# A three-layer fp32 kernel on one core: the prologue of its attention is reordered, and its weight conversions come 16 slots later

## The chip, the cores and the metric

One core of a Trainium2 chip runs one program with three layers in it. The metric is device time in microseconds of one execution; lower is better. The profile names the engines PE (TensorE, matmuls) with PEld (its weight loads), DVE (VectorE), ACT (ScalarE), POOL (GpSimd) and SP (SyncE, which here does nothing but issue DMAs). SPq and ACTq are DMAs issued from SyncE's and from ScalarE's instruction stream.

## The reference, cut to what matters

Inputs are fp32; the weights of the second layer, `w_in` and `w_out`, arrive as 8-byte floats, of which the kernel makes fp32 itself.

```python
# q, k, v: (2, 8, 768, 64); centroids: (8, 16, 64)
q_assign = np.argmax(einsum(normalised q, normalised centroids), axis=-1)   # 16 clusters
k_assign = ...                                                             # the same for k
mask = q_assign[:, :, :, None] == k_assign[:, :, None, :]
scores = np.where(mask, scale * q @ k.T, -1e9)
scores = scores - scores.max(-1, keepdims=True)
attn = np.exp(scores); attn /= attn.sum(-1, keepdims=True) + 1e-9
x = (attn @ v) reshaped to (1536, 512)
x = (s * relu(x @ w_in) ** 2 + b) @ w_out        # d_ff 2048
# then a mixture of 8 experts on x, one expert a row, d_ff 1024
```

## The kernel before, in words

**Attention, head by head.** There are 16 heads of 768 rows. A head is prepared in these steps, each a small function inside `attention`:

- `load` (L117): SyncE loads q and k (and, apart, v) of 192 KB each.
- `split` (L145): ScalarE rounds q or k to the fast fp32r type (the high part, L150), GpSimd (for head 0 VectorE) subtracts to get the low part (L152).
- `trans` (L157): three TensorE transposes into the PSUM bank `t`, one ScalarE copy out of it (L168); four such groups a head, two for k and two for q. After the second of each, SyncE copies the high half into `ka` or `qa` by DMA (L170).
- `sims_mm` and `sims_a` to `sims_e` (L174 to L203): similarities with the centroids on TensorE into one PSUM bank, then six VectorE instructions that find the cluster of each row.
- `masks` (L205): a VectorE transpose turns the clusters into extra rows of `qa` and `ka` (tile `ot`, L208). In heads 0 and 1 the four pieces are copied by ScalarE (L216) and VectorE (L218), two each; from head 2 on SyncE sends them by four DMAs (L212, L214).
- `M` (L220): 12 score matmuls a head, each followed by a VectorE maximum over its 384 columns (L224). In head 0 they rotate over five PSUM banks, later over two.
- `mneg`, `mrow` (L228, L232): the negated row maxima, turned into a row by a TensorE matmul (`mr`, L235), a ScalarE copy (`mrs`, L237) and a small SyncE DMA into `qa` (L238).

Only with that row in `qa` can the head's own 12 score pairs `Sx` start (L247, L248; the exponentials on ScalarE, L249; two PSUM banks `s0`, `s1`), then `V` (attn times v), `presum` (GpSimd adds the exponentials) and the normalisation.

**What sets the order.** Every function is put into a list with a time in slots, `at(t, f, ...)`; the list is sorted by that time, and each engine's instructions are pinned to the order that comes out. A slot is no measure of time, only a rank. Head j's first score matmul `Sx` has slot 12j, so 12 slots are a head; all its other steps have an offset from there in the table `TIMES` (L31). Thus M of head j stands at slots 12j - 17.4 to 12j - 6.4 and its maxima row at 12j - 3.5 (head 0: -5.6). `HEAT` (L35) puts idle bf16 matmuls (`heat`, L1133) into the prologue, and two more behind each M of head 0.

**The hooks of the second layer** (`Moe.hooks`, L393) stand in the same list. `fetch` (L401) loads the raw weights of blocks 0, 1 and 2, 1 MB each in two DMAs, from ScalarE's stream, at slots 5.3, 17.3 and 29.3 (`FETCH`). `conv_steps` (L416) converts block f in steps at slots 36f + 12 + `CONV`: two ScalarE absolute values (L422), then seven VectorE instructions on integers; the last step, at 36f + 43.2, loads the raw block f + 3 into the buffers just freed. Of these loads, block 3's is issued by ScalarE and those of blocks 4, 5 and 6 by SyncE. Block 4 is converted at slots 176.2 and after. `early` (L396) fills constants and loads two scalars at slot 6.3; `unit` and `project` prepare the expert embedding.

The second layer (`moe1`) and the experts follow, with their matmuls in three passes of fp32r parts.

Of the kernel before, what the change touches and what calls it, by code (L numbers as in the profile page):

```python
# [9 lines left out]
F32 = mybir.dt.float32  # L10
# [5 lines left out]
AF = mybir.ActivationFunctionType  # L16
# [5 lines left out]
P = 128  # L22
# [3 lines left out]
HS = S // 2  # L26
# [2 lines left out]
MASK = float(2 ** 33)  # L29
GUARD = 1e-9  # L30
TIMES = dict(load=-49, loadv=-18, split=(-42, -40), trans=(-36.6, -35.6, -33.6, -32.6), sims=-30.53, simv=(-26.5, -26.5, -26.5, -22.52, -22.52, -22.51),  # L31
             M=-17.4, mneg=-5.7, mrow=-3.5, V=(5.45, 5.45, 9.45, 9.45, 13.45, 13.45), presum=3.0, norm=(14.5, 25.47, 29.5, 29.5, 29.5))
ENDS = {14: (14.5, 21.47, 22.4, 23.4, 24.4), 15: (14.5, 14.6, 14.7, 14.8, 14.9)}
WARM = -26
HEAT = ((-41, 7), (-30.5, 6), (-22, 6))  # L35
SETUP, FETCH = 6.3, (5.3, 17.3, 29.3)
CONV = (3.2, 7.2, 11.2, 15.2, 19.2, 23.2, 27.2, 31.2)
F, DM, TC = 2048, 512, 512
NF, KD, NTT = F // P, DM // P, TC // P
E, F2 = 8, 1024  # L40
NWA = 5
# [50 lines left out]


def attention(ax, tc, cst, q, k, v, cen, xt, hooks, embed):
    nc = tc.nc
    ident, identr, ones, desc, cc, ps = cst.ident, cst.identr, cst.ones64, cst.desc, cst.cc, cst.ps
    io = ax.enter_context(tc.tile_pool(name="io", bufs=3))
    w1 = ax.enter_context(tc.tile_pool(name="w1", bufs=2))
# [4 lines left out]
    NSET, NPB = 4, 8  # L103
    qa = [ab.tile([P, S], F32R, name=f"qa{i}") for i in range(NSET)]
    ka = [ab.tile([P, S], F32R, name=f"ka{i}") for i in range(NSET)]
# [66 lines left out]
    si, sm = {}, {}  # L172
# [31 lines left out]

    def masks(j):  # L205
        i = j % NSET
        ot = w1.tile([P, HS], F32, name="ot", tag="ot")
        nc.vector.transpose(out=ot, in_=si.pop(j))  # L208
        for g in range(4):
            da, w = (qa, ka)[g // 2][i], slice(g % 2 * HS, (g % 2 + 1) * HS)  # L210
            if j >= NSET:
                nc.sync.dma_start(out=da[64:64 + NC_, w].bitcast(F32), in_=ot[32 * g:32 * g + NC_])  # L212
            elif j > 1:
                nc.sync.dma_start(out=da[64:96, w].bitcast(F32), in_=ot[32 * g:32 * g + 32])  # L214
            elif g % 2 == 0:
                nc.scalar.activation(out=da[64:96, w], in_=ot[32 * g:32 * g + 32], func=AF.Copy)  # L216
            else:
                nc.vector.tensor_copy(da[64:96, w], ot[32 * g:32 * g + 32])  # L218

    def M(j, r, c):  # L220
        i = j % NSET
        pp = ps([P, HS], "M", f"M{c}" if j else ("M0", "M1", "s0", "s1", "s2")[(2 * r + c) % 5])
        nc.tensor.matmul(pp, qa[i][0:80, r * P:(r + 1) * P], ka[i][0:80, c * HS:(c + 1) * HS])  # L223
        nc.vector.tensor_reduce(out=mxt[j % 2][:, r, c:c + 1], in_=pp, axis=AX.X, op=ALU.max)  # L224
# [90 lines left out]
    c = w1.tile([P, D], F32, name="c", tag="c")  # L315
# [8 lines left out]
    n = order.mark()  # L324
# [12 lines left out]
    def at(t, f, *a):  # L337
        ops.append((t, len(ops), f, a))

    at(WARM, lambda: nc.scalar.activation(out=cst.warm, in_=cst.ones64[0:1, 0:1], func=AF.Exp, scale=0.0))  # L340
    at(-31, cluster, ch)
    for t, n in HEAT:
        at(t, cst.heat, n, "pv")
    at(-30, lambda: [nc.sync.dma_start(out=ka_[96:97, :].bitcast(F32), in_=one) for ka_ in ka])
    for t, f in hooks:
        at(t, f)
    T = TIMES
    for j in range(NH):
        o = 12 * j
        if j >= 3:  # L350
            at(o + T["load"], load, j, "qk")
            at(o + T["loadv"], load, j, "v")
        if j > 0:
            for i in range(2):
                at(o + T["split"][i], split, j, i)
        for i in range(4):
            at(o + T["trans"][i], trans, j, "kq"[i // 2], i % 2)
        at(o + T["sims"], sims_mm, j)
        for i, f in enumerate((sims_a, sims_b, sims_c, sims_d, sims_e, masks)):
            at(o + T["simv"][i], f, j)  # L360
        for r in range(NR):
            for c in range(2):
                at(o + T["M"] + 2 * r + c, M, j, r, c)
                if j == 0:
                    at(o + T["M"] + 2 * r + c, cst.heat, 2, "pv")
        at(o + T["mneg"], mneg, j)
        at(o + T["mrow"] if j else -5.6, mrow, j)
        for t in range(NR):
            for c in range(2):
                at(o + 2 * t + c, Sx, j, t, c)  # L370
            at(o + T["V"][t], V, j, t)
            at(o + 2 * t + T["presum"], presum, j, t)
        for i, f in enumerate((pv_out, sums, norm_a, norm_b, norm_c)):
            at(o + ENDS.get(j, T["norm"])[i], f, j)
    for t, _, f, a in sorted(ops, key=lambda x: x[:2]):
        n = order.mark()
# [4 lines left out]
class Moe:  # L381
# [11 lines left out]
    def hooks(self, ms, mb):  # L393
        nc = self.nc

        def early():  # L396
            for i, t in enumerate((ms, mb)):
                nc.sync.dma_start(out=self.sb[:, i:i + 1], in_=t.rearrange("(o n) -> o n", o=1).to_broadcast([P, 1]))
            self.setup()

        def fetch(f):  # L401
            self.loaded[f] = self.load_f64(f, nc.scalar)

        self.loaded, self.wT, self.wraw, self.running = {}, {}, {}, {}
        out = [(-27, self.length), (SETUP, early), (-16.6, self.unit), (SETUP + 9, self.project)] + [(t, lambda f=f: fetch(f)) for f, t in enumerate(FETCH)]
        for f in range(NWA):
            for n, t in enumerate(CONV):
                out.append((36 * f + 12 + t if f < NWA - 1 else 176.2 + n, lambda f=f: next(self.steps(f), None)))
        return out

    def steps(self, f):
# [4 lines left out]
    def conv_steps(self, f, wide=False):  # L416
        nc = self.nc
        r = self.loaded.pop(f)
        t = self.w32(f, U32)
        u = [self.ps([P, DM], "cv", "ab"[a]).bitcast(U32) if wide else t[:, a] for a in range(2)]  # L420
        for a in range(2):
            nc.scalar.activation(out=t[:, a].bitcast(F32), in_=r[a][:, :, 1].bitcast(F32), func=AF.Abs)  # L422
        yield
        s = t.rearrange("p a (w o) -> p o (a w)", o=2)
        nc.vector.tensor_scalar(out=s.bitcast(F32), in0=s.bitcast(F32), scalar1=CLAMP_LO, scalar2=CLAMP_HI, op0=ALU.max, op1=ALU.min)
        yield
        shift = dict(scalar1=5, scalar2=2, op0=ALU.logical_shift_left, op1=ALU.logical_shift_right)
        if wide:
            for a in range(2):
                nc.vector.tensor_scalar(out=u[a], in0=t[:, a], **shift)  # L430
        else:
            nc.vector.tensor_scalar(out=s, in0=s, **shift)
        yield
        for a in range(2):
            nc.vector.scalar_tensor_tensor(out=u[a], in0=r[a][:, :, 1], scalar=0xC0000000, in1=u[a], op0=ALU.bitwise_and, op1=ALU.bitwise_or)
            yield
            nc.vector.scalar_tensor_tensor(out=t[:, a], in0=r[a][:, :, 0], scalar=29, in1=u[a], op0=ALU.logical_shift_right, op1=ALU.bitwise_or)
            yield
        self.wT[f] = t
        if f + 3 < NF:  # L440
            self.loaded[f + 3] = self.load_f64(f + 3, nc.scalar if f + 3 < NWA - 1 else nc.sync)
        yield

    def pools(self):
# [12 lines left out]
    def ps(self, shape, name, tag):  # L457
        return self.cst.ps(shape, name, dict(a="pv", b="sm", y0="t", y1="s0", y2="s1", y3="s2").get(tag, tag))
# [124 lines left out]
    def moe1(self, xt):  # L583
# [4 lines left out]
        for c in range(self.chunks):  # L588
# [4 lines left out]
            def up(f):  # L593
# [4 lines left out]
                if final:  # L598
                    self.load_expert(f + 1)
                    if f in PRE0:  # L600
                        z = PRE0.index(f)
                        with self.after(*tail):
                            self.pre0[z] = self.half(self.wraw[0, z], 0, nc.gpsimd, False)
                hp = self.ps([P, TC], "hp", f"M{f % 2}")
                self.up_mm(hp, *wu, lambda k: x[k // 2][:, k % 2], lambda k: x[2 + k // 2][:, k % 2])
# [434 lines left out]
    def prep(self, xr):  # L1040
# [12 lines left out]
        return xh, xl  # L1053

    def block(self, y, args, w, pre, hooks, wd=None, g0=None):
        nc = self.nc
        xh, xl, off, _ = args
# [5 lines left out]
        def up(f):  # L1063
            with ExitStack() as behind:
# [5 lines left out]
                if f not in wd:  # L1070
                    wd[f] = self.half(w[f], 1, nc.vector)
            hp = self.ps([P, T], "hp", f"M{f % 2}")
            if xl is None:
# [79 lines left out]
@with_exitstack  # L1153
def tile_kernel(ctx, tc, q, k, v, cen, w_in, w_out, ms, mb, emb, tau, w1, w2, out):
    nc = tc.nc
    cst = consts(ctx, tc)
    xp = ctx.enter_context(tc.tile_pool(name="xp", bufs=1))
    xt = [xp.tile([P, KD, TC], F32, name="xt", tag=f"xt{i}") for i in range(NT // TC)]
    sb = cst.pool.tile([P, 2], F32, name="sb")
    moe = Moe(ctx, tc, cst, w_in, w_out, sb, emb, tau, w1, w2, out)  # L1160

    with ExitStack() as ax:
        attention(ax, tc, cst, q, k, v, cen, xt, moe.hooks(ms, mb), moe.embed)
    moe.pools()
    moe.xp = xp
    moe.moe1(xt)
    moe.spare = [xp.tile([P, KD, TC], dt, name="spare", tag=f"xt{i}") for i, dt in enumerate((F32R, F32R, F32))]
    moe.experts()
# [26 lines left out]
```

## Time and profile before

| what | value |
|---|---|
| times of three runs | 810.01, 814.52, 817.02 us; median 814.52 us |
| the profiled execution | 812.13 us |
| its span, first to last instruction | 810.3 us |
| mean granted TensorE clock over the span | 0.971 |
| busy PE / DVE / ACT / POOL | 764.7 / 521.3 / 422.0 / 347.6 us |
| first score matmul of head 0, of head 15 | 35.85 us, 274.74 us |
| last score matmul of the attention | 288.81 us |

The span is what the trace shows; 1.83 us of the profiled execution's time lie around it. Busy time is an average over stages with different limits. Matmuls are pipelined and their ends are modelled, so a busy TensorE is not necessarily one at its peak. In the views below, the text in brackets behind an instruction is the idle time of its engine just before it and what ended that.

### The profile page before, as it was taken

What the parts mean: (1) busy time and instruction counts of PE and PEld (TensorE: products, weight loads), DVE (VectorE), ACT (ScalarE), POOL (GpSimd) and SP (SyncE); (2) the same over time, 40 slices, a digit from 0 to 9 for tenths busy, and PEclk for the clock granted to TensorE, in tenths of its full rate; (3) what the DMA queues carried; (4) which work ended last, traced back from release to release, by engine and by line L of the source; (5) the groups of instructions that cost most, each with busy time, mean ns of one, the idle gap of its engine ahead of it and who ended that gap; (6) DMA issues with size and microseconds to landing.
All of it is one profiled execution on the core that took longest, in us unless ns stands there. A gap on an engine that the chain in (4) does not pass through costs nothing. (4 is left out here: it accounts for less than half of the span.)

```text
span 810.3 us, 12231 instructions
## 1 busy us (share of the span) xinstructions
PE 764.7 (94%) x4193; PEld 578.5 (71%) x4193; DVE 521.3 (64%) x1087; ACT 422.0 (52%) x841; POOL 347.6 (43%) x277
## 2 busy tenths in 40 slices
PE   7799999898998889999999999989999999999994
PEld 3456555554555458888788887868879998989883
DVE  5769789795995779994353542556447545757750
ACT  5355465554553665645435553445437545756651
POOL 2067766675684655445344544437042202220000
PEclk9899999998998999999999999989999999999998
DMA  5155423424331205521000042254132754876600
GB/s 149 50 148 171 126 69 87 141 75 120 76 81 58 61 22 159 183 74 45 8 1 1 1 155 79 81 205 156 66 117 69 255 178 139 245 248 227 213 17 23
DMA packets 75470, 88.73 MB, mean 110 GB/s; under 512 B 7445, under 2 KB 58549, under 8 KB 75008
## 3 DMA queue, kind: packets, MB, share of 16 engines
q1 hardware_dynamic: 68704, 69.67, 28.2%
q0 software_dynamic: 4000, 13.90, 5.4%
q10 hardware_dynamic: 2688, 4.19, 1.7%
q8 instruction: 40, 0.66, 0.3%
q14 instruction: 38, 0.31, 0.1%
HBM read 70.57 MB, written 7.34 MB: 96 GB/s over the span
## 5 line engine op out<-in xcount | busy, mean ns | idle before, releaser
L531 POOL TENSOR_TENSOR wl<-w,wh 128x512 fp32r<-128x512 f32 x96 | 123.2, 1308 | 130.5 <-ACT wh L529 127.9
L249 ACT ACTIVATE pt<-S 128x384 f32<-128x384 f32 x192 | 91.7, 490 | 120.3 <-PE S L248 115.7
L224 DVE TENSOR_REDUCE mx<-M 128x1 f32<-128x384 f32 x192 | 101.8, 551 | 50.8 <-PE M L223 48.7
L260 POOL TENSOR_TENSOR acc<-acc,pt 128x768 f32<-128x768 f32 x61 | 106.1, 1739 | 6.5 <-ACT pt L249 4.1
L552 PE MATMUL hp<-x,wh 128*128 128x512 f32 x384 | 105.9, 397 | 0.5 <-ACT wh L529 0.5
L552 PE MATMUL hp<-x,spare 128*128 128x256 f32 x732 | 96.1, 284 | 2.0 <-PEq L987 1.7
L552 PEld LDWEIGHTS hp<-x,spare 128*128 128x128 f32 x732 | 92.7, 190 | 6.9 <-issue 4.1
L560 PE MATMUL y<-wd,gg 128*128 128x512 f32 x360 | 93.2, 394 | 0.0
L608 DVE SCALAR_TENSOR_TENSOR hp<-hp,sb,t 128x512 f32<-128x512 f32 x48 | 36.3, 757 | 75.3 <-ACT t L607 75.2
L247 PE MATMUL S<-qa,ka 97*128 97x384 f32 x192 | 72.7, 379 | 12.7 <-DMA qa<-mrs 11.0
L223 PE MATMUL M<-ka,qa 80*128 80x384 f32 x192 | 79.4, 414 | 3.5 <-DVE mx L224 2.2
L552 PEld LDWEIGHTS hp<-x,wh 128*128 128x128 f32 x384 | 71.2, 189 | 15.5 <-ACT wh L529 1.2
L268 PE MATMUL pv<-pt,vn 128*64 128x385 f32 x384 | 77.3, 526 | 0.0
L560 PE MATMUL y<-wh,gh 128*128 128x512 f32 x192 | 75.3, 392 | 0.0
L560 PE MATMUL y<-wl,gh 128*128 128x512 f32 x192 | 75.2, 392 | 0.0
L545 DVE TENSOR_TENSOR wd<-w,wd 128x512 fp32r<-128x512 f32 x64 | 43.3, 686 | 44.4 <-ACT wd L544 41.0
L560 PEld LDWEIGHTS y<-wd,gg 128*128 128x128 f32 x360 | 63.7, 189 | 10.1 <-DVE gg L1084 0.2
L1036 POOL DMA_INDIRECT row<-rows,idx x24 | 28.0, 1166 | 94.1 <-PE tp L1048 50.8
L248 PE MATMUL S<-qb,kb 128*128 128x384 f32 x192 | 66.9, 349 | 0.0
L607 ACT ACTIVATE t<-hp 128x512 f32<-128x512 f32 x48 | 28.8, 599 | 72.1 <-PE hp L552 72.1
L223 PEld LDWEIGHTS M<-ka,qa 80*128 80x128 f32 x192 | 37.1, 194 | 37.8 <-DVE su L296 8.1
L560 PE MATMUL y<-wh,gl 128*128 128x512 f32 x192 | 59.5, 391 | 0.0
(269 smaller groups left out, 1363.2 us busy)
## 6 DMA issues: line engine op xcount, KB each, us to landing
w<-in_moe_w_dram SPq DMA_DIRECT2D x128, 256.0 KB
raw<-in_moe_w_in_dram SPq DMA_DIRECT2D x12, 512.0 KB
raw<-in_moe_w_out_dram SPq DMA_DIRECT2D x12, 512.0 KB
qn<-in_q_dram SPq DMA_DIRECT2D x16, 192.0 KB
kn<-in_k_dram SPq DMA_DIRECT2D x16, 192.0 KB
vn<-in_v_dram SPq DMA_DIRECT2D x16, 192.0 KB
ka<-kb SPq DMA_DIRECT2D x16, 192.0 KB
qa<-qb SPq DMA_DIRECT2D x16, 192.0 KB
```

The lines of the kernel that those rows point to most:

```text
L223: nc.tensor.matmul(pp, qa[i][0:80, r * P:(r + 1) * P], ka[i][0:80, c * HS:(c + 1) * HS])
L224: nc.vector.tensor_reduce(out=mxt[j % 2][:, r, c:c + 1], in_=pp, axis=AX.X, op=ALU.max)
L247: nc.tensor.matmul(pp, ka[i][0:97, t * P:(t + 1) * P], qa[i][0:97, w], start=True, stop=False)
L248: nc.tensor.matmul(pp, kb[i][:, t * P:(t + 1) * P], qb[i][:, w], start=False, stop=True)
L249: exps.setdefault((j, t), []).append(nc.scalar.activation(out=p[:, c, 0:HS], in_=pp, func=AF.Exp, scale=0.125).ins)
L260: eng.tensor_tensor(out=acc[j][-1], in0=acc[j][-1], in1=p[:, :, 0:HS], op=ALU.add)
L268: together(tc, [lambda c=c: nc.tensor.matmul(pv_t[j][c * 64:c * 64 + 64, :], io_t["v", j][:, t, :], p[:, c, :], start=t == 0, stop=t == NR ...
L531: eng.tensor_tensor(out=wl[:, a], in0=w[:, a], in1=wh[:, a].bitcast(F32), op=ALU.subtract)
L545: eng.tensor_tensor(out=t[:, 1], in0=w[:, a], in1=t[:, 0].bitcast(F32), op=ALU.subtract)
L552: self.nc.tensor.matmul(hp, a[:, k * P:(k + 1) * P], b(k), start=n == 0, stop=n == 3 * KD - 1)
L560: self.nc.tensor.matmul(y[i], (gl if n == 2 else gh)[:, s], wl if n == 1 else wh, start=first and n == 0, stop=last and n == 2)
L608: nc.vector.scalar_tensor_tensor(out=hp, in0=hp, scalar=sb[:, 0:1], in1=t, op0=ALU.mult, op1=ALU.mult)
```

## The change

Heads 0 to 4 get tables of their own (`FIRST`) in place of `TIMES`:

- Head 0's twelve M stand directly behind its masks (slots -22.4 to -18.0, one heat behind each, where there were two at -17.4 to -6.4), its maxima row at -17.8.
- Head 1's similarities and masks come earlier (masks at -17.3), its M later, at 2.1 to 7.6 (before: -5.4 to 5.6), its maxima row at 8.2.
- Head 2's transposes start at 0.4 (before -12.6), its masks come at 8.1 (before 1.49), its M at 11.6 to 19.85 (before 6.6 to 17.6). Its four mask pieces are copied by VectorE and ScalarE, as those of heads 0 and 1, and no longer by DMA.
- Head 3's transposes start at 6.6 (before -0.6), its M stand at 21.6 to 30.95 (before 18.6 to 29.6); its q and k are loaded at -30 (before -13). Head 4's similarities come at 21.47 (before 17.47).
- ScalarE's two mask copies are a function `copies` with a slot of its own: -22.51 in head 0, 0.5 for head 1 and 11.4 for head 2.
- The heats of the prologue are 7, 16 and 10 (before 7, 6 and 6).
- `early` moves from 6.3 to -16.5, `project` from 15.3 to 20.3, the three fetches to 11.2, 23.2 and 35.2.
- The conversions of blocks 0 to 3 begin at 36f + 28 in place of 36f + 12, and their two absolute values have a slot each. So the loads of blocks 3 to 6 stand at slots 59.2, 95.2, 131.2 and 167.2 (before 43.2, 79.2, 115.2, 151.2), and ScalarE issues all four.

```diff
-HEAT = ((-41, 7), (-30.5, 6), (-22, 6))
-SETUP, FETCH = 6.3, (5.3, 17.3, 29.3)
-CONV = (3.2, 7.2, 11.2, 15.2, 19.2, 23.2, 27.2, 31.2)
+FIRST = {0: dict(TIMES, M=(-22.4, 0.4), mneg=-17.85, mrow=-17.8),
+         1: dict(TIMES, trans=(-36.6, -34.2, -33.4, -32.6), sims=-31.5, simv=(-29.5, -29.5, -29.5, -29.4, -29.4, -29.3), copies=-11.5, M=(-9.9, 0.5), mneg=-4.2, mrow=-3.8),
+         2: dict(TIMES, split=(-42, -41.5), trans=(-23.6, -22.6, -21.4, -20.6), sims=-18.53, simv=(-16, -16, -16, -16, -16, -15.9), copies=-12.6, M=(-12.4, 0.75), mneg=-3.9),
+         3: dict(TIMES, load=-66, split=(-33, -31), trans=(-29.4, -28.4, -27.4, -25.6), sims=-22.53, simv=(-21.9, -21.1, -20.3, -19.5, -19.4, -18.7), M=(-14.4, 0.85), mneg=-4.4),
+         4: dict(TIMES, sims=-26.53, simv=(-25.5, -25.5, -25.5, -22.52, -22.52, -22.51))}
+HEAT = ((-41, 7), (-30.5, 16), (-17.7, 10))
+SETUP, FETCH = -16.5, (11.2, 23.2, 35.2)
+CONV = (3.2, 5.2, 7.2, 11.2, 15.2, 19.2, 23.2, 27.2, 31.2)
...
-            elif j > 1:
+            elif j > 2:
                 nc.sync.dma_start(out=da[64:96, w].bitcast(F32), in_=ot[32 * g:32 * g + 32])
-            elif g % 2 == 0:
-                nc.scalar.activation(out=da[64:96, w], in_=ot[32 * g:32 * g + 32], func=AF.Copy)
-            else:
+            elif g % 2:
                 nc.vector.tensor_copy(da[64:96, w], ot[32 * g:32 * g + 32])
+
+    def copies(j):
+        for g in (0, 2):
+            nc.scalar.activation(out=(qa, ka)[g // 2][j % NSET][64:96, 0:HS], in_=sm[j][32 * g:32 * g + 32], func=AF.Copy)
...
-        at(o + T["mrow"] if j else -5.6, mrow, j)
+        at(o + T["mrow"], mrow, j)
...
-                out.append((36 * f + 12 + t if f < NWA - 1 else 176.2 + n, lambda f=f: next(self.steps(f), None)))
+                out.append((36 * f + 28 + t if f < NWA - 1 else 176.2 + n, lambda f=f: next(self.steps(f), None)))
...
             nc.scalar.activation(out=t[:, a].bitcast(F32), in_=r[a][:, :, 1].bitcast(F32), func=AF.Abs)
-        yield
+            yield
...
-        self.loaded[f + 3] = self.load_f64(f + 3, nc.scalar if f + 3 < NWA - 1 else nc.sync)
+        self.loaded[f + 3] = self.load_f64(f + 3, nc.scalar if f < NWA - 1 else nc.sync)
```

## Rows read from the trace of the kernel before

**Rows 1.** The page: the span, and TensorE's busy tenths in 40 equal slices.

```profile
span 810.3 us, 12231 instructions
PE   7799999898998889999999999989999999999994
```

**Rows 2.** Busy time by stretch: the prologue, then heads by their first score matmul.

```profile
core 0: us, PE busy (x) PEld busy (x) DVE busy (x) ACT busy (x) POOL busy (x), PEclk, DMA share, GB/s
0.00:35.85 35.85, 25.44 (x126) 12.44 (x127) 24.31 (x64) 16.15 (x36) 7.98 (x25) 0.91 0.38 107
35.85:49.81 13.96, 13.91 (x74) 9.76 (x74) 9.65 (x33) 7.69 (x18) 5.97 (x10) 0.88 0.49 133
...
80.40:96.96 16.56, 14.85 (x86) 9.00 (x86) 14.35 (x30) 8.66 (x22) 12.36 (x9) 1.00 0.49 150
96.96:113.73 16.77, 16.42 (x86) 9.88 (x86) 11.51 (x26) 9.27 (x23) 9.22 (x7) 0.90 0.29 72
...
128.93:146.17 17.24, 14.80 (x86) 8.85 (x86) 14.38 (x30) 8.70 (x22) 13.11 (x9) 1.00 0.47 134
...
161.38:176.56 15.18, 14.84 (x87) 8.98 (x86) 14.20 (x30) 8.40 (x22) 11.16 (x8) 1.00 0.33 86
176.56:194.58 18.02, 14.80 (x87) 8.85 (x86) 14.40 (x30) 8.73 (x22) 13.83 (x10) 0.95 0.46 135
194.58:212.15 17.57, 17.23 (x86) 10.32 (x87) 11.51 (x26) 9.26 (x23) 7.77 (x6) 0.85 0.27 68
...
227.37:245.69 18.32, 14.65 (x84) 8.56 (x83) 14.37 (x30) 7.71 (x19) 13.56 (x8) 0.96 0.38 107
```

**Rows 3.** Line 247 (the score matmuls): one releaser of its engine's idle time.

```profile
  DMA qa<-mrs: 11.0, 5
```

**Rows 4.** Timeline around heads 4 and 10: weight load, maxima row, first score matmul.

```profile
90.92 0.41 ACTq L522 DMA_DIRECT2D raw<-in_moe_w_in_dram  x1
...
93.06 0.76 SPq L238 DMA_DIRECT2D qa<-mrs  x1
...
96.96 0.41 PE L247 MATMUL S<-qa,ka 97*128 97x384 f32 x1 [1.51 <-DMA qa<-mrs]
...
188.27 0.45 SPq L522 DMA_DIRECT2D raw<-in_moe_w_in_dram  x1
...
189.37 0.78 SPq L238 DMA_DIRECT2D qa<-mrs  x1
...
194.58 0.66 PE L247 MATMUL S<-qa,ka 97*128 97x384 f32 x1 [3.01 <-DMA qa<-mrs]
```

**Rows 5.** Busy time in one microsecond of head 10 after that wait.

```profile
195.00:196.00 1.00, 1.00 (x6) 0.90 (x6) 0.00 (x0) 0.35 (x1) 1.00 (x1) 0.50 0.00 0
```

**Rows 6.** Timeline of the prologue.

```profile
8.48 1.47 PE L1133 MATMUL heat<-work 128*128 128x512 bf16 x6
...
11.61 0.58 DVE L208 STREAM_TRANSPOSE ot<-si 128x384 f32<-128x384 f32 x1
...
12.23 0.52 ACT L216 ACTIVATE qa<-ot 32x384 fp32r<-32x384 f32 x1 [0.52 <-DVE ot L208]
...
15.86 0.69 PE L223 MATMUL M<-ka,qa 80*128 80x384 f32 x1
...
21.80 1.94 DVE L224 TENSOR_REDUCE mx<-M 128x1 f32<-128x384 f32 x4
...
30.47 0.22 PE L235 MATMUL mr<-identr,mn 128*6 128x128 f32 x1 [0.41 <-DVE mn L230]
...
31.03 0.81 SPq L238 DMA_DIRECT2D qa<-mrs  x1
```

**Rows 7.** Groups by line on ScalarE, to 290 us: busy, mean ns | idle before.

```profile
L249 ACT ACTIVATE pt<-S 128x384 f32<-128x384 f32 x192 | 91.7, 490 | 120.3 <-PE S L248 115.7 <-POOL acc L260 2.5 <-PE mr L235 0.9
L168 ACT ACTIVATE qb<-tp 128x384 fp32r<-128x384 f32 x32 | 15.5, 489 | 1.1 <-PE tp L162 1.1
L150 ACT ACTIVATE ks<-kn 128x384 fp32r<-128x384 f32 x16 | 8.3, 519 | 1.5 <-DMA kn<-in_k_dram 1.4
```

**Rows 8.** Timeline of an undisturbed head: its predecessor's row, masks, first M behind them.

```profile
166.71 1.21 SPq L212 DMA_DIRECT2D ka<-ot  x2
...
170.43 0.44 PE L223 MATMUL M<-ka,qa 80*128 80x384 f32 x1
...
173.60 0.75 SPq L238 DMA_DIRECT2D qa<-mrs  x1
```

More of the change, by code (lines that the diff above doesn't have):

```diff
@@ L31 @@
 TIMES = dict(load=-49, loadv=-18, split=(-42, -40), trans=(-36.6, -35.6, -33.6, -32.6), sims=-30.53, simv=(-26.5, -26.5, -26.5, -22.52, -22.52, -22.51),
-             M=-17.4, mneg=-5.7, mrow=-3.5, V=(5.45, 5.45, 9.45, 9.45, 13.45, 13.45), presum=3.0, norm=(14.5, 25.47, 29.5, 29.5, 29.5))
+             M=(-17.4, 1), mneg=-5.7, mrow=-3.5, V=(5.45, 5.45, 9.45, 9.45, 13.45, 13.45), presum=3.0, norm=(14.5, 25.47, 29.5, 29.5, 29.5))
 ENDS = {14: (14.5, 21.47, 22.4, 23.4, 24.4), 15: (14.5, 14.6, 14.7, 14.8, 14.9)}
 WARM = -26
-HEAT = ((-41, 7), (-30.5, 6), (-22, 6))
-SETUP, FETCH = 6.3, (5.3, 17.3, 29.3)
-CONV = (3.2, 7.2, 11.2, 15.2, 19.2, 23.2, 27.2, 31.2)
+FIRST = {0: dict(TIMES, M=(-22.4, 0.4), mneg=-17.85, mrow=-17.8),
[6 more added lines that the diff above has]
+CONV = (3.2, 5.2, 7.2, 11.2, 15.2, 19.2, 23.2, 27.2, 31.2)
 F, DM, TC = 2048, 512, 512
@@ L206, in masks @@
         i = j % NSET
-        ot = w1.tile([P, HS], F32, name="ot", tag="ot")
+        ot = sm[j] = w1.tile([P, HS], F32, name="ot", tag="ot")
         nc.vector.transpose(out=ot, in_=si.pop(j))
@@ L346, in attention @@
         at(t, f)
-    T = TIMES
     for j in range(NH):
         o = 12 * j
+        T = FIRST.get(j, TIMES)
         if j >= 3:
@@ L360, in attention @@
             at(o + T["simv"][i], f, j)
+        if j < 3:
+            at(o + T.get("copies", T["simv"][5]), copies, j)
         for r in range(NR):
             for c in range(2):
-                at(o + T["M"] + 2 * r + c, M, j, r, c)
+                first, step = T["M"]
+                at(o + first + step * (2 * r + c), M, j, r, c)
                 if j == 0:
-                    at(o + T["M"] + 2 * r + c, cst.heat, 2, "pv")
+                    at(o + first + step * (2 * r + c), cst.heat, 1, "pv")
         at(o + T["mneg"], mneg, j)
-        at(o + T["mrow"] if j else -5.6, mrow, j)
+        at(o + T["mrow"], mrow, j)
         for t in range(NR):
@@ L404, in hooks @@
         self.loaded, self.wT, self.wraw, self.running = {}, {}, {}, {}
-        out = [(-27, self.length), (SETUP, early), (-16.6, self.unit), (SETUP + 9, self.project)] + [(t, lambda f=f: fetch(f)) for f, t in enumerate(FETCH)]
+        out = [(-27, self.length), (SETUP, early), (-16.6, self.unit), (20.3, self.project)] + [(t, lambda f=f: fetch(f)) for f, t in enumerate(FETCH)]
         for f in range(NWA):
             for n, t in enumerate(CONV):
-                out.append((36 * f + 12 + t if f < NWA - 1 else 176.2 + n, lambda f=f: next(self.steps(f), None)))
+                out.append((36 * f + 28 + t if f < NWA - 1 else 176.2 + n, lambda f=f: next(self.steps(f), None)))
         return out
```

## The prediction

> **What bounds the kernel now.** I read the page's slices first, then a table of busy time by stretch, then the waits of single lines, then the timeline where a wait stands. The slices show TensorE busy eight tenths and more from the third slice to the last but one [rows 1]: the layers behind the attention are its own work, the change does not touch them, and whatever the attention ends earlier or later they move along. So only the attention is left, about 290 us. The table shows two losses in it. First, head 0's first score matmul comes at 35.85 us, with TensorE busy for 25.44 of them, heats included [rows 2]. Second, an undisturbed head takes 15.18 us, TensorE busy for 14.84 and VectorE for 14.20 of them; six heads (3 and 4, 6, 9 and 10, 12, counted by the first score matmul that opens them) take 16.56 to 18.32 [rows 2]. In heads 3, 6, 9 and 12 TensorE's busy time is still 14.65 to 14.85, so it is waiting at their ends. For what, the score line says: 11.0 us in five waits end with the DMA that brings a head's maxima row into `qa` [rows 3]. The timeline says why that row is late: 1.1 to 2.1 us before it was issued, a raw weight block of 1 MB was issued, and the score matmul waits 1.51 us (head 4) or 3.01 us (head 10) [rows 4]. After the long wait the granted clock reads 0.50 [rows 5], the lower of its two levels (1.2 in place of 2.4 GHz), so the head behind the wait is slower too (17.57 us at 0.85) [rows 2].
>
> The slots say that this is systematic: a weight load stands at 36f + 43.2 and a maxima row at 36f + 44.5, in heads 4, 7, 10 and 13, just where the long heads are.
>
> **The change, part by part**, against the profiled execution (812.13 us, span 810.3).
>
> *A: head 0's first score matmul.* Its masks end on VectorE at 11.61 + 0.58 = 12.19 [rows 6], and nothing ahead of them on VectorE moves. But ScalarE's two mask copies are queued behind the copy of head 1's first transposes, and these now stand behind 16 heats in place of 6. Six took 1.47 [rows 6], so 16 take 3.9, from 8.48 to 12.4; transposes and copy at about 0.5 each [rows 7] give 13.4, the two mask copies at 0.52 [rows 6] 14.4. If the heats run denser, 13.3; before, the first M was at 15.86. Now the twelve maxima: VectorE makes four in 1.94 [rows 6], so twelve in 5.8. TensorE has between them twelve heats, three groups of transposes, each waiting for ScalarE to empty the one bank, and head 1's similarities, so I take 6.3, and the ends are 5.8 and 9. That is 20.7. The row: 30.47 to 31.03 from its matmul to its DMA issue [rows 6], some 0.8 with the maximum ahead of it; from issue to the score matmul at most 176.56 - 173.60 = 2.96 where nothing waited [rows 2, 8], and I take 3. So 20.7 + 0.8 + 3 = 24.5 (22.5 to 28): **A = -11.3** (-13.4 to -8). The ten heats behind the row lie in that wait and cost nothing; without them the clock could fall there. SyncE is passed by head 3's loads, issued early into buffers that are free, and by the two scalars of `early`, both with nobody waiting; `early` on VectorE and GpSimd stands where head 1's M are still to come.
>
> *B: the work that is put behind it.* Head 0's own twelve slots now hold twelve M of head 1, eight groups of transposes, head 2's similarities and two pairs of mask copies. On ScalarE that is 12 exponentials at 0.490, 8 copies at 0.489, 4 splits at 0.519 [rows 7], 4 mask copies at 0.52 [rows 6], the row's copy and a fetch's two issues (one 0.41 [rows 4]), together some 1.2: 5.9 + 3.9 + 2.1 + 2.1 + 1.2 = 15.2 us. ScalarE, at 7.69 busy of 13.96 before [rows 2], is full in this head, and as it also waits I take 15.8: +1.8. Head 1 gets three M and one similarity more than a steady head (+0.8), head 2 three M (+0.4). VectorE has room, since the conversions start only at slot 31. **B = +3.0**; the lower end is +1, when it all fits TensorE's gaps, the upper +8, when ScalarE's queue also starves TensorE and the clock falls as in rows 5.
>
> *C: the weight loads.* They now stand at 36f + 59.2, so 2.7 slots behind a maxima row and 9.3 ahead of the next; the fetches at 11.2 likewise stand behind the rows at 8.2, 20.5 and 32.5. In an undisturbed head the row is issued 2.96 us before its score matmul and the load would be issued about 1 us before it, so the row has about 2 us start. The excess over 15.18 of the six heads shown is 1.38 + 1.59 + 2.06 + 2.84 + 2.39 + 3.14 = 13.4 [rows 2]: **C = -13.4** (to -9, if some waits of a microsecond stay).
>
> That ScalarE issues all four loads is priced at nothing. Head 4's load was issued by ScalarE already, and its two heads lost 3.0 us; one issued by SyncE cost 2.1 (head 7), one 5.2 (head 10) [rows 2, 4]. The Trainium skill agrees (DMA: Bandwidth & Descriptors, "Issuing engines are not separate DMA queues": DMAs from whichever engine run on the same 16 engines and interleave); by it, C would be 0 if only the queue moved and not the slot, and the sum 804.8.
>
> *D: where the load lands instead.* It is in flight from about the first score matmul on; in head 10 a load issued at 188.27 let the score matmul go at 194.58, so 6 us [rows 4]. In that time the mask pieces of a later head are issued: their last issue ends at 166.71 + 1.21 = 167.92, 6.5 us behind the head's first score matmul at 161.38, and the first M that reads them is at 170.43 [rows 2, 8], so 2.5 us of slack against a tail of the load. ScalarE's two issues (0.9) stand in front of an exponential. The VectorE steps of the conversion move by 16 slots, so by four within a head, where other VectorE work stands. Seven loads at 0.15 each: **D = +1.0** (-1 to +7, a microsecond for each load).
>
> Sum: -11.3 + 3.0 - 13.4 + 1.0 = -20.7, so 791.4 against the profiled execution. The median of the three runs stands 2.4 above it, and their spread is 7; I put the forecast half a microsecond up and say **792 us**.
>
> **The rivals.**
>
> *The collision only moves (slower, or not faster).* The row is spared, but each of seven 1 MB transfers now meets the mask pieces, and the first M of the head waits in TensorE's queue with all score matmuls behind it. For it: the masks are issued within the load's 6 us. Against it: the 2.5 us of slack. The Trainium skill's sentence on issuing engines (DMA: Bandwidth & Descriptors, the section above) speaks for it too: the small transfers share the engines with the large one whichever queue it came from. At the price of head 10 with its successor, 2.84 + 2.39 = 5.2 a load, it is 7 x 5.2 = 36.4: 812.1 - 11.3 + 3.0 - 13.4 + 36.4 = 826.8. It makes the kernel slower from 21.7 / 7 = 3.1 us a load on. Chance 0.05.
>
> *The catch-up eats the prologue's gain.* Work put behind the first score matmul has to be done all the same, on engines that are near full; B reaches 11 through ScalarE in head 0, a late row for head 1, and a low clock. Left is C with D: 812.1 - 13.4 + 1.0 = 799.7. For it: ScalarE's 15.2 us of work in a head of 15. Against it: TensorE idles or heats for more than 10 us of the old prologue, and it is TensorE that limits the later heads. Chance 0.20.
>
> *The waits stay.* The maxima row is late for another cause than the load (SyncE's queue, the row's own small packets), so C is nothing and the rest holds: 812.1 - 11.3 + 3.0 + 1.0 = 804.8. Against it: undisturbed heads issue the same row the same way with no wait, and head 10's wait ends as the transfer does. Chance 0.10.
>
> **How the numbers follow.** The forecast has 0.65. A measurement of this kernel tells about 1% (8 us) from no change. Faster by more than that: the forecast, the second rival, and a good third of the last (804.8 lies at the edge): 0.65 + 0.20 + 0.03 = 0.88. Within 1%: the rest of the last, 0.07. Slower: 0.05. The range: below, A, B and D at their good ends together give 812.1 - 13.4 + 1 - 13.4 - 1 = 785.3; above, it takes in the second rival and most of the third, 805.
>
> **What would show it.** Right: head 0's first score matmul at 22.5 to 28 us; its head 15 to 17 us with ScalarE nearly full; heads 4, 7, 10 and 13 at 15.2 each with their successors; no wait of the score line on the maxima row over 1 us; head 4's first score matmul near 87 us (before 96.96), head 13's near 225 (before 245.69); the granted clock at its upper level from head 1 to head 13. Wrong: a new idle before an M with a DMA of `ot` named, a head 0 of 20 us, or rows still late beside a load that is now 9 slots away. If the attention ends 20 us earlier and the span doesn't, then the second layer was waiting for something else.

## The result, and the profile after

The changed kernel takes 802.96 us (median of four runs, 802.33 to 804.92); the kernel before, on the same chip, 815.77. The ratio is 0.986 (95% interval 0.9818 to 0.9901): faster, but by 12.8 us where the forecast stood 20 below the profiled time. The profiled executions are 812.13 and 803.02 us, so 9.1 apart; the terms below are worked out in these two.

The head of the page after, which answers to [rows 1], with the tenths of the granted TensorE clock under TensorE's busy tenths:

```profile
span 801.2 us, 12227 instructions
PE   7888999999999899999999999989999999999994
PEclk9999999999999999999999999999999999999998
```

Behind the attention nothing is new, as expected: from the last score matmul (288.81 us before, 281.23 after) to the end of the span it is 521.5 and 520.0 us, and in the experiments below 518 to 521.5 whatever was changed. So the attention is again the only place to look. Busy time by stretch, cut as in [rows 2] with the same columns: the prologue; head 0; two stretches of 5 us about its end; heads 1 and 2; head 4; heads 3 to 14 together; three heads of the steady part.

```profile
0.00:25.77 25.77, 20.34 (x100) 9.70 (x100) 17.05 (x42) 11.79 (x27) 6.40 (x25) 0.93 0.43 118
25.77:45.58 19.81, 15.75 (x90) 9.64 (x90) 16.57 (x47) 13.13 (x30) 13.29 (x14) 1.00 0.31 76
...
40.00:45.00 5.00, 2.66 (x18) 1.41 (x14) 4.74 (x7) 2.68 (x7) 4.84 (x4) 1.00 0.34 76
45.00:50.00 5.00, 4.70 (x18) 2.70 (x18) 2.47 (x4) 1.72 (x4) 0.58 (x1) 0.66 0.99 313
...
45.58:63.41 17.83, 17.26 (x97) 10.14 (x96) 10.76 (x26) 8.16 (x20) 7.23 (x6) 0.90 0.44 131
63.41:84.96 21.55, 19.15 (x92) 10.26 (x91) 15.40 (x35) 9.82 (x24) 11.76 (x8) 0.84 0.37 110
...
101.11:116.30 15.19, 14.85 (x86) 8.98 (x86) 14.20 (x30) 8.33 (x21) 11.16 (x8) 1.00 0.34 87
...
84.96:266.80 181.84, 173.50 (x973) 103.75 (x972) 154.74 (x319) 101.70 (x247) 124.67 (x79) 1.00 0.36 100
...
147.61:193.85 46.24, 44.72 (x256) 26.92 (x256) 40.24 (x85) 26.69 (x66) 32.77 (x22) 1.00 0.38 107
```

And the same cut of the kernel before, from head 3's first score matmul to head 15's:

```profile
80.40:274.74 194.34, 179.56 (x973) 107.02 (x972) 152.02 (x317) 100.48 (x247) 127.02 (x80) 0.96 0.33 89
```

Head 0's first score matmul comes 10.08 us earlier (25.77 for 35.85). Heads 0 to 2 then take 59.19 us, where they took 80.40 - 35.85 = 44.55, so head 3 starts 4.56 *later* than before. From there on heads 3 to 14 take 12.50 less, at the upper level of the clock throughout. Head 15 and what follows give 1.1 more. Sum: -10.1 + 14.6 - 12.5 - 1.1 = -9.1. The whole gain is made in the heads whose waits went; the prologue's ten microseconds were spent, and more, before head 3.

That the waits went is one row. The score matmuls' idle time put down to the maxima row was 11.0 us in five waits [rows 3]; after:

```profile
  DMA qa<-mrs: 1.0, 2
```

The timeline of the changed kernel at the end of head 0 (start, duration, engine, line, operation; in brackets the engine's idle time before it), and at the end of head 2:

```profile
40.39 5.19 POOL L267 TENSOR_TENSOR acc<-acc,pt 128x768 f32<-128x768 f32 x3
42.21 1.83 DVE L221 CAST qa<-ot 32x384 fp32r<-32x384 f32 x1
42.29 0.43 ACTq L532 DMA_DIRECT2D raw<-in_moe_w_in_dram  x1
42.66 0.42 PE L167 MATMUL tp<-identr,ks 128*128 128x128 f32 x3 [0.41 <-ACT qb L173]
42.76 0.51 ACTq L533 DMA_DIRECT2D raw<-in_moe_w_out_dram  x1
43.69 0.49 ACT L173 ACTIVATE kb<-tp 128x384 fp32r<-128x384 f32 x1 [0.79 <-PE tp L167]
44.06 1.74 DVE L221 CAST ka<-ot 32x384 fp32r<-32x384 f32 x1
44.19 0.52 ACT L225 ACTIVATE qa<-ot 32x384 fp32r<-32x384 f32 x1
44.73 0.52 ACT L225 ACTIVATE ka<-ot 32x384 fp32r<-32x384 f32 x1
45.30 0.44 PE L230 MATMUL M<-ka,qa 80*128 80x384 f32 x1 [2.22 <-ACT ka L225]
...
84.70 0.39 ACTq L532 DMA_DIRECT2D raw<-in_moe_w_in_dram  x1
85.13 0.52 ACTq L533 DMA_DIRECT2D raw<-in_moe_w_out_dram  x1
85.69 0.49 ACT L173 ACTIVATE kb<-tp 128x384 fp32r<-128x384 f32 x1 [0.50 <-PE S L255]
86.23 0.45 PE L167 MATMUL tp<-identr,ks 128*128 128x128 f32 x3 [0.77 <-ACT kb L173]
```

Two waits of TensorE on ScalarE are to be seen. The first M of head 2 waits 2.22 us for ScalarE's two mask copies: the masks were transposed by 42.2, when VectorE's own casts of them begin, but ScalarE first issued a weight fetch (42.29 and 42.76) and then stood in order before a transpose copy, which was itself waiting for TensorE. The last row shows the smaller kind: a transpose copy behind two DMA issues, and TensorE 0.77 us idle for it. In the 5 us around the first of these TensorE is busy for 2.66, and in the next 5 the granted clock reads 0.66. Behind the prologue three such falls to the lower level (1.2 in place of 2.4 GHz) begin, at 45.9, 66.3 and 80.0 us.

### The profile page after: what moved, and what is told of

The parts are those of the page before. It is cut to its first block, busy times and chain, and to the rows that moved or that the text cites. A ratio compares the mean times of both kernels' runs of the same rounds, so it can differ in the third digit from the quotient of the medians.

```text
span 801.2 us, 12227 instructions
## 1 busy us (share of the span) xinstructions
PE 760.6 (95%) x4195; PEld 573.4 (72%) x4195; DVE 525.6 (66%) x1089; ACT 423.9 (53%) x843; POOL 346.8 (43%) x277
## 5 line engine op out<-in xcount | busy, mean ns | idle before, releaser
L230 PE MATMUL M<-ka,qa 80*128 80x384 f32 x192 | 77.3, 409 | 8.6 <-ACT ka L225 4.1
L562 PEld LDWEIGHTS hp<-x,wh 128*128 128x128 f32 x384 | 71.2, 189 | 15.4 <-ACT wh L539 1.1
```

What stands on the lines that cost most here:

```text
L562: self.nc.tensor.matmul(hp, a[:, k * P:(k + 1) * P], b(k), start=n == 0, stop=n == 3 * KD - 1)
```

## The experiments

Times are medians, ratios are against the kernel before on the same chip, with 95% intervals. "Heads 3 to 14" is the stretch between the first score matmuls of heads 3 and 15 in the profiled execution. With the loads out of the rows' way it repeats well: kernels that then differ only ahead of it agree in it within 0.4 us, while whole runs of one kernel spread by 1 to 8 us, so parts of a microsecond are read from the stretches.

**The two halves of the change.** The kernel before with the later conversions and fetches alone, loads by ScalarE (`CONV` and the place of `yield`, cut here, are as in the change):

```diff
-SETUP, FETCH = 6.3, (5.3, 17.3, 29.3)
+SETUP, FETCH = 6.3, (11.2, 23.2, 35.2)
...
-                out.append((36 * f + 12 + t if f < NWA - 1 else 176.2 + n, lambda f=f: next(self.steps(f), None)))
+                out.append((36 * f + 28 + t if f < NWA - 1 else 176.2 + n, lambda f=f: next(self.steps(f), None)))
...
-            self.loaded[f + 3] = self.load_f64(f + 3, nc.scalar if f + 3 < NWA - 1 else nc.sync)
+            self.loaded[f + 3] = self.load_f64(f + 3, nc.scalar if f < NWA - 1 else nc.sync)
```

> The kernel before with nothing but the later conversions, fetches and loads (by ScalarE); the prologue is the old one. Theory 1 (the reordered prologue gives back its ten microseconds, and more, by head 3, and the whole gain is the weight loads'): head 3's first score matmul near 80.4 us as before, no wait on the maxima row over 1 us, about 13 us under the kernel before and some 3 to 5 us under the changed kernel: 797 to 800 us. Rival (the later loads are what slows heads 0 to 2, because ScalarE issues the fetches in front of transpose copies): heads 1 and 2 over 17 us here too, head 3 near 85, and 803 us or more.

Measured: 802.03 us, 0.9849 (0.9793 to 0.9905). Head 3 starts at 83.35, heads 3 to 14 take 181.50.

The changed kernel with these lines put back (`SETUP` stays at -16.5), so the new prologue alone:

> The changed kernel with conversions, fetches and loads where they were before. Theory 1: head 3's first score matmul at 83 us or later (before 80.4), the waits on the maxima row in heads 4, 7, 10 and 13 as before, so 815 to 822 us, not faster than before. Rival (the prologue alone is worth what the prediction gave it, and it is the later loads that spoil it): head 3 near 73 us and about 806 us.

Measured: 823.39 us, 1.0106 (1.0055 to 1.0157). The score line's waits on the maxima row, and the stretch of heads 3 to 14:

```profile
  DMA qa<-mrs: 12.6, 6
...
89.60:288.65 199.05, 183.03 (x973) 107.74 (x972) 150.99 (x316) 100.88 (x247) 123.71 (x78) 0.94 0.32 86
```

The loads' half gives the whole gain by itself. The prologue's half begins head 0 at 24.30, reaches head 3 at 89.60, and with the loads still in the rows' way it makes the kernel slower. The halves do not add up: against the kernel before (814.55 beside both) they are -12.5 and +8.8, and together they are -12.8. Heads 0 to 2 take 65.30 here and 59.19 in the change, so the later fetches and conversions also relieve the new prologue's catch-up; and heads 3 to 14 take 4.7 more here than in the kernel before.

**Who issues the loads.** The changed kernel with all but the first of the conversions' loads back on SyncE:

```diff
-            self.loaded[f + 3] = self.load_f64(f + 3, nc.scalar if f < NWA - 1 else nc.sync)
+            self.loaded[f + 3] = self.load_f64(f + 3, nc.scalar if f + 3 < NWA - 1 else nc.sync)
```

> The changed kernel with the loads of blocks 4 to 6 issued by SyncE as before, at the new slots. If only the slot counts: within 1.5 us of the changed kernel (803). Rival (a load in SyncE's own queue stands in front of the mask pieces and the transposes' DMAs, which are issued there after it): heads 7, 10 and 13 longer by 1 us or more each, with waits on DMAs of the masks, and 806 us or more.

Measured: 800.83 us, 0.9833 (0.9785 to 0.988), from the change not to be told apart in the time. The trace tells: the three steady heads shown above in 46.24 us take

```profile
149.28:194.81 45.53, 44.48 (x256) 26.87 (x256) 40.23 (x85) 26.44 (x66) 32.78 (x22) 1.00 0.40 108
```

0.7 less for the one load in them.

**The copies behind the fetch.** The changed kernel with head 2's mask copies one slot earlier, ahead of the fetch's issues:

```diff
-         2: dict(TIMES, split=(-42, -41.5), trans=(-23.6, -22.6, -21.4, -20.6), sims=-18.53, simv=(-16, -16, -16, -16, -16, -15.9), copies=-12.6, M=(-12.4, 0.75), mneg=-3.9),
+         2: dict(TIMES, split=(-42, -41.5), trans=(-23.6, -22.6, -21.4, -20.6), sims=-18.53, simv=(-16, -16, -16, -16, -16, -15.9), copies=-13.55, M=(-12.4, 0.75), mneg=-3.9),
```

> The changed kernel with ScalarE's two mask copies of head 2 one place earlier: ahead of the last exponential, the fetch and a transpose copy; all other engines' orders are the same. Theory (the 2.2 us in which the first M of head 2 waits for these copies, and the fall of the clock behind it, are due to what stands in front of them on ScalarE): that wait under 1 us, head 0 some 1.5 to 2 us shorter (19.8 to about 18), head 1 at the clock's upper level throughout, 3 to 4 us in all: 799 to 800 us. Rival (VectorE's two mask copies, 1.8 us each beside GpSimd's additions, hold the same M's maximum anyway): the wait moves to VectorE and the time stays within 1 us of 803.

Measured: 799.87 us, 0.9824 (0.9769 to 0.9879). Heads 0 to 2 by stretch, the timeline at the end of head 0, and TensorE's waits in these three heads (line, releaser, us in total, times, longest):

```profile
25.69:43.85 18.16, 15.74 (x89) 9.63 (x90) 14.94 (x46) 12.58 (x29) 11.63 (x13) 1.00 0.25 58
43.85:60.43 16.58, 15.96 (x97) 9.32 (x96) 10.95 (x27) 8.63 (x22) 8.93 (x7) 1.00 0.57 168
60.43:78.89 18.46, 16.06 (x91) 9.54 (x90) 15.06 (x34) 9.97 (x24) 10.33 (x7) 1.00 0.39 116
```

```profile
40.31 3.44 POOL L267 TENSOR_TENSOR acc<-acc,pt 128x768 f32<-128x768 f32 x2
42.14 1.82 DVE L221 CAST qa<-ot 32x384 fp32r<-32x384 f32 x1
...
43.57 0.44 PE L230 MATMUL M<-ka,qa 80*128 80x384 f32 x1 [0.56 <-ACT ka L225]
43.98 0.35 DVE L221 CAST ka<-ot 32x384 fp32r<-32x384 f32 x1
44.18 1.70 POOL L267 TENSOR_TENSOR acc<-acc,pt 128x768 f32<-128x768 f32 x1 [0.43 <-ACT pt L256]
44.39 0.44 PE L230 MATMUL M<-ka,qa 80*128 80x384 f32 x1
44.67 0.38 PE L167 MATMUL tp<-identr,ks 128*128 128x128 f32 x3
```

```profile
PE M L230 <- DVE mx L231: 1.9, 4, 0.7
PE tp L167 <- ACT kb L173: 1.3, 3, 0.6
PE M L230 <- ACT ka L225: 0.8, 2, 0.6
PE mr L242 <- DVE mn L237: 0.6, 2, 0.4
PE tp L167 <- ACT qb L173: 0.4, 1, 0.4
PE tp L167 <- ACT vm L283: 0.2, 1, 0.2
```

The wait of 2.22 is 0.56, head 0 is 1.65 shorter, and the clock did not fall in heads 0 to 2 of this execution: head 3 starts at 78.89. The waits that are left are short ones, thirteen of them for 5.2 us, on VectorE and ScalarE in turn; TensorE's busy time is 15.74 + 15.96 + 16.06 = 47.76 of 53.20.

The same with fetches and loads by SyncE:

```diff
-            self.loaded[f] = self.load_f64(f, nc.scalar)
+            self.loaded[f] = self.load_f64(f, nc.sync)
...
-            self.loaded[f + 3] = self.load_f64(f + 3, nc.scalar if f < NWA - 1 else nc.sync)
+            self.loaded[f + 3] = self.load_f64(f + 3, nc.sync)
```

> The kernel with the mask copies of head 2 ahead of the fetch, and with all fetches and loads issued by SyncE in place of ScalarE, at the same slots. Theory (ScalarE's two issues, 0.9 us, stand in front of a transpose copy and TensorE waits 0.6 to 0.8 us for it; that is the 0.3 us by which heads with a load behind them are longer): six loads at 0.7 us less, heads 3 to 12 at 15.2 or less each: 3 to 5 us under the kernel with ScalarE's loads (799.9), so 795 to 797 us. Rival (the fetches in SyncE's queue stand in front of head 3's mask pieces and hold their M): a gain under 1 us or a loss.

Measured: 797.96 us, 0.9821 (0.9773 to 0.9869); heads 3 to 14 in 178.79 in place of 181.69.

And with ScalarE still issuing, but 0.3 of a slot later, behind the transpose copy that TensorE waits for:

```diff
-SETUP, FETCH = -16.5, (11.2, 23.2, 35.2)
-CONV = (3.2, 5.2, 7.2, 11.2, 15.2, 19.2, 23.2, 27.2, 31.2)
+SETUP, FETCH = -16.5, (11.5, 23.5, 35.5)
+CONV = (3.2, 5.2, 7.2, 11.2, 15.2, 19.2, 23.2, 27.2, 31.5)
```

> The kernel with the mask copies of head 2 ahead of the fetch; ScalarE still issues all fetches and loads, but 0.3 slots later, behind the first transpose copy in place of in front of it; nothing else changes place. Theory (the cost of ScalarE's issues is only that one copy standing behind them, for which TensorE waits 0.6 to 0.8 us): heads with a load at their end go from 15.5 to 15.2 and below, and the time is that of the kernel with SyncE's loads, 797 to 798 us against 799.9. Rival (the issues hold ScalarE whatever stands next, or the transfer itself slows the heads): 15.5 stays, within 1 us of 799.9.

Measured: 798.12 us, 0.9795 (0.9757 to 0.9833); heads 3 to 14 in 179.30. So nearly all of what the issues cost was their place in ScalarE's queue. But in this profiled execution the clock fell three times and head 3 came at 83.55. Its timeline where the one above goes on without a fall, and the stretches on both sides:

```profile
43.57 0.44 PE L230 MATMUL M<-ka,qa 80*128 80x384 f32 x1 [0.56 <-ACT ka L225]
...
44.38 0.45 PE L230 MATMUL M<-ka,qa 80*128 80x384 f32 x1
44.66 0.51 PE L167 MATMUL tp<-identr,ks 128*128 128x128 f32 x3
```

```profile
40.00:44.50 4.50, 3.50 (x20) 1.94 (x16) 4.21 (x8) 2.84 (x7) 3.99 (x4) 1.00 0.27 58
44.50:49.50 5.00, 5.00 (x24) 2.31 (x25) 1.49 (x3) 1.26 (x3) 1.37 (x1) 0.66 0.95 311
```

From head 0's first score matmul to 44.66 TensorE's work in the two stands within 0.02 us; there the three transposes take 0.51 in place of 0.38, and the clock reads 0.66. The execution that kept its clock shows the same 3.50 us of busy time from 40.00 to 44.50. Ahead of head 0 the two differ: the mean granted clock of the prologue is 0.93 in the one that kept its clock later and 1.00 in the other. Head 3 comes 83.55 - 78.89 = 4.66 later with three falls in heads 0 to 2 than with none, 1.55 a fall.

**Is it the early M, or what was put off for them?** The changed kernel with a table for head 0 alone; heads 1 to 4 keep their old slots, and head 2's masks come by DMA again (the prologue's heats, `early` and the later loads stay as in the change):

```diff
-FIRST = {0: dict(TIMES, M=(-22.4, 0.4), mneg=-17.85, mrow=-17.8),
...
+FIRST = {0: dict(TIMES, M=(-22.4, 0.4), mneg=-17.85, mrow=-17.8)}
...
-            elif j > 2:
+            elif j > 1:
...
-        if j < 3:
+        if j < 2:
```

> One part of the change alone on top of the later loads: head 0's M directly behind its masks; heads 1 to 4 keep the old table, with head 2's mask pieces by DMA. Theory (it is the work of heads 1 to 4 put behind the first score matmul that costs the prologue's gain): first score matmul near 30 us (old prologue 36 to 38, the change 25.8), heads 0 to 2 at 14 to 15.8 us each, head 3 near 76 (the change 84.96, with earlier mask copies 78.89): 794 to 797 us. Rival (the early M of head 0 themselves hold up the other heads' preparation): first score matmul at 33 or later, or heads 0 to 2 over 17: no better than 800 us.

Measured: 803.37 us, 0.9872 (0.9833 to 0.9912). The prologue's stretch and one row of its timeline:

```profile
0.00:40.55 40.55, 27.58 (x129) 13.87 (x129) 25.73 (x76) 16.34 (x36) 9.28 (x31) 0.82 0.35 94
```

```profile
32.12 0.62 PE L163 MATMUL tp<-identr,qs 128*128 128x128 f32 x3 [3.15 <-ACT qb L169]
```

Head 0's score matmuls come *later* than before (40.55): its early M push the others' preparation back, and the clock is at 0.82. The row shows it: these transposes of head 2 begin at 32.12 behind a wait of 3.15, and in the kernel before at 26.68 behind one of 2.49. Putting heads 1 to 4 off is not an ornament of the change; without it the early M gain nothing. With all loads by SyncE this kernel gave:

> The kernel with only head 0's part and the later loads, with fetches and loads issued by SyncE. Theory: both gains add up, 2 to 4 us under the same kernel with ScalarE's loads: 791 to 794 us. Rival: with head 2's mask pieces by DMA again, the 1 MB fetches ahead of them in SyncE's queue hold the first M of heads 2 and 3 by a microsecond or more each, and nothing is gained.

802.35 us, 0.9867 (0.9828 to 0.9907); first score matmul at 41.73, heads 3 to 14 in 178.93.

**Is the serial passage through one bank the cause?** The transposes of a head all go through one PSUM bank, emptied by ScalarE. The kernel with early copies and SyncE's loads, k's second transposes in another bank:

```diff
-        pp = ps([P, HS], "tp", "t" if j else ("t", "s0", "s1", "s2")[2 * (nm == "q") + c], F32R)
+        pp = ps([P, HS], "tp", ("s2" if j > 1 and (nm, c) == ("k", 1) else "t") if j else ("t", "s0", "s1", "s2")[2 * (nm == "q") + c], F32R)
```

> The kernel with earlier mask copies and SyncE's loads; the second group of k's transposes of heads 2 and up goes to another PSUM bank, so that TensorE need not wait for ScalarE's copy of the first. Theory (part of what is left of the catch-up is TensorE standing in its own order behind ScalarE's copies out of the one bank): heads 0 to 2 together 1.5 to 3 us shorter (54.8 to about 52.5), steady heads 0 to 0.4 us: 794 to 797 us. Rival (TensorE's own work and VectorE's maxima bound these heads): under 1 us, 797 to 798 us.

Measured: 792.48 us, 0.9737 (0.9698 to 0.9776). Heads 3 to 14 without and with the second bank:

```profile
80.68:259.47 178.79, 172.94 (x973) 103.74 (x972) 154.60 (x320) 101.09 (x247) 126.34 (x79) 1.00 0.37 103
```

```profile
83.24:260.31 177.07, 171.66 (x973) 104.21 (x972) 154.21 (x319) 100.09 (x247) 124.16 (x78) 1.00 0.37 101
```

Heads 3 to 14 gain 1.7; the catch-up does not. Head 1, at the upper level of the clock in both, takes 16.54 for the 16.58 of the kernel with early copies; head 2 in the last kernel below, which has the second bank too, takes 18.45 for 18.46. Head 3 starts at 83.24 with two falls of the clock, in the slowest of this kernel's six executions. So one of the four groups in another bank does not shorten heads 0 to 2; the other three were not tried.

**Old prologue against new.** The kernel of the first experiment with all loads by SyncE, without and with the second bank:

> The kernel before with the later conversions, fetches and loads, these issued by SyncE: the old prologue at its best, to set the new one against. Theory (the new prologue as changed is worth nothing, and 2 to 5 us with the mask copies moved): head 3 near 81 to 83 us, 799 to 801 us, so 2 to 4 above the kernel with earlier mask copies and SyncE's loads (798.0). Rival (the reordered prologue is worth nothing in either form): 797 to 798 us.

> The old prologue with the later loads by SyncE and the second bank for k's second transposes: the counterpart of the same loads and bank on the new prologue (792.5). Theory (the second bank's gain is in the steady heads with a load at their end, 15.5 to 15.15, some 2 us in all, whatever the prologue): 794 to 795 us against 796.5 without the bank, and 2 us above the new prologue with it. Rival (the bank's gain was in the catch-up): no gain here, 796 to 797 us.

Measured: 796.5 us, 0.9783 (0.975 to 0.9816), heads 3 to 14 in 179.00; and 795.89, 0.976 (0.9713 to 0.9806), in 177.20. Old against new prologue: with ScalarE's loads 802.03 and 802.96; with SyncE's 796.5 and 797.96, the latter with the early copies too (the 800.83 without them is no fair partner, as ScalarE issues its fetches and first load); with the bank 795.89 and 792.48, whose intervals overlap.

**The last one** takes the kernel with early copies, SyncE's loads and the second bank and moves `early` and `unit` behind head 1's first M:

```diff
-SETUP, FETCH = -16.5, (11.2, 23.2, 35.2)
+SETUP, FETCH = 5.5, (11.2, 23.2, 35.2)
...
-        out = [(-27, self.length), (SETUP, early), (-16.6, self.unit), (20.3, self.project)] + [(t, lambda f=f: fetch(f)) for f, t in enumerate(FETCH)]
+        out = [(-27, self.length), (SETUP, early), (5.2, self.unit), (20.3, self.project)] + [(t, lambda f=f: fetch(f)) for f, t in enumerate(FETCH)]
```

> The new prologue with earlier mask copies, SyncE's loads and the second bank, and with the expert embedding's and the constants' VectorE work (about 2 us) moved from in front of head 1's first maxima to slots 5.2 and 5.5, where VectorE was idle. Theory (VectorE's queue in front of head 1's first maximum makes TensorE wait 0.5 to 0.8 us early in head 0, and such waits in a row bring the clock down): head 0 at 17.5 to 18 us, the clock falls in fewer executions (mean granted clock of the runs 0.987 or more in most), median 789 to 792 us against 792.5. Rival (head 0 is bound by the chain through its masks and the moved work is in the way of head 1's last maxima and row instead): head 0 as long or longer, no gain.

Measured: 793.5 us, 0.9746 (0.9696 to 0.9797): no gain; head 0 takes 21.27 at a mean clock of 0.84.

The lowest median of the study is that of the second bank on the new prologue: 792.48 us, under both the kernel before and the changed one. The two other kernels with that bank, at 795.89 and 793.5, can't be told apart from it.

## Why the prediction was wrong

*A, head 0's first score matmul (24.5): held.* It came at 25.77, in the range given, -10.1 for -11.3. Two errors in it partly cancel, which is luck: the twelve maxima end at 23.05 for 20.7, and the row with its way into `qa` takes 2.7 for 3.8.

*B, the work put behind it (+3.0): this is the step that failed.* It cost +14.6, past its own upper end of +8. Against the forecast's 71.9 for head 3's start (24.5 + 15.8 + 16.0 + 15.6) the 84.96 is 13.1 late: 1.3 from A; 1.65 from the mask copies behind a fetch; some 4.3 that the kernel with early copies, which had no fall of the clock in these heads, did not lose (the kernel that issues behind the copy lost 4.66 to three falls, and the runs of either lie 4.6 us and more apart); and 5.8 that is left when both are gone, 53.20 against 47.4. The last part names the error. TensorE's busy time in those heads is 47.76, so its *work* alone would have fitted the forecast. But I took a head to last as long as its fullest engine is busy, and thought that engine to be ScalarE, at 15.2. In head 0 ScalarE is busy for 13.13 of 19.81, VectorE, to which I had given room, for 16.57 (2.9 of them two casts that wait, as the last section shows), TensorE for 15.75: none is full. The postponed work is a chain, in order on each engine, that passes from TensorE to ScalarE or VectorE and back, and each passage costs a wait of 0.2 to 0.7 us. A steady head pays 0.34 of them (15.19 less 14.85); heads 0 to 2, with more of the chain in each, pay 5.4. "Behind" the score matmuls was not "beside" them. The thirteen waits are what the trace shows; that the chain as such makes them, and not one link of it, is argued from them, and no experiment took them away.

*C, the weight loads (-13.4), and D, where the load lands (+1.0): together right by luck, each off.* Heads 3 to 14 gave -12.5 for -12.4. But with the loads on SyncE the stretch is 178.8 to 179.0, so moving the loads is worth some 15.4, and ScalarE's issuing them gives 2.5 to 2.9 back. Heads 4, 7 and 10 take 15.19 to 15.21, as forecast; heads 6, 9 and 12, in which no load stands either, take 15.5, and 15.1 with the second bank.

*"That ScalarE issues all four loads is priced at nothing": wrong, by the same 2.5 to 2.9.* The 0.9 us of issue stands in front of a transpose copy that TensorE waits for, not in front of an exponential. The queue mattered not for the transfer but for the engine that issues. The Trainium skill (DMA: Bandwidth & Descriptors, "Issuing engines are not separate DMA queues") says so too, and calls the sequencer's time usually small relative to the DMA; here it was small beside the transfer (0.9 us of issue, 3.6 and 4.8 us from issue to landing) and still cost 0.7 a load.

*The rivals.* The second, that the catch-up eats the prologue's gain, is what happened; its 799.7 let the prologue come out at nothing, and here head 3 starts 4.6 later than before. Of its three causes the low clock is seen; ScalarE is late by its order, not by being full; a late row for head 1 is not seen, since none of TensorE's waits in heads 0 to 2 ends with a DMA. The first did not come about: no M waits for a mask piece's DMA. Nor did the third: the rows' waits went with the loads.

*What was to show it.* Of the signs named beforehand, head 0's first score matmul and the score line's wait came out right; "a head 0 of 20 us" stood among the signs of wrong, and it is 19.81. Head 4's first score matmul is at 101.11 and not near 87, head 13's at 240.12 and not near 225; the clock is 0.90 and 0.84 in heads 1 and 2.

What stays open: what decides, between two executions with the same order of TensorE's work, whether the clock falls; and how a new prologue would have to be written so that its ten microseconds reach head 3. By the three comparisons of the old prologue with the new, the reordering is worth between a loss of 1.5 us and a gain of 3.4 by the medians, a loss of 3 and a gain of 2 by the ratios, which can't be told from nothing.

## What to carry to other kernels

A start that comes earlier is worth only what is left of it where the steady part begins: price the catch-up as a chain, with a wait at each passage between engines, not as the busy time of the fullest one. Moving a large load out of the way of a small one that gates an engine is the safe half of such a change; take each half alone before crediting either, and do not expect the halves to add up. A DMA issue costs its engine's queue, so look at which instruction stands behind it, and who waits for that.

## What had not been expected of the hardware

VectorE's casts of 32x384 take 0.35 us in the two other heads that have them, and 1.83 and 1.74 in the changed kernel's head 0, while GpSimd adds (40.39 to 45.58). In the kernel with early copies the first takes 1.82 beside GpSimd's additions, and the second, begun at 43.98 between two of them (43.75 and 44.18), 0.35. The Trainium skill (GPSIMD Engine Reference, "8. Key points") says that GpSimd shares its SBUF interfaces with VectorE, with contention for VectorE's instructions in a 2-port mode or with two SBUF inputs. These rows show contention, a factor of five in a cast's time; whether the casts are of one of these forms they don't show. Each long cast ends 0.2 us behind the end of an addition (44.04 for 43.83 and 45.80 for 45.58; in the kernel with early copies 43.96 for 43.75), so the factor looks like a wait for that addition, not like a slower cast.

The clock fell behind stretches with many short waits of TensorE (3.50 busy of 4.50 us, above), not only behind one long one as in [rows 5], and in one execution and not in another of the same order of work on TensorE. The six runs of the second bank on the new prologue show the same spread: 798.06 and 797.91 us at a mean granted clock of 0.981 and 0.983, the other four 790.09 to 793.0 at 0.987 to 0.993.
